# Choosing batch 0's expert from summed state rows, and re-spacing the side work, in a fused attention and switch-routing kernel

## The chip, the cores and the metric

The kernel runs on one NeuronCore of one Trainium2 chip. The metric is the device time of one execution in microseconds (us); the time before is the median of three runs. A profile is one execution recorded by the hardware profiler; its times count from the first instruction of the program.

## The reference

Two blocks follow each other. The first is a two-way cross attention between 512 tokens `x` and 32 states per batch and head (8 batches, 8 heads, 64 channels). Its result, 544 rows of 512 channels per batch, goes into a mixture of 8 experts in which every row uses one expert.

```python
# attention, per batch and head
a  = softmax(x @ state.T / 8);   xread = a  @ state     # 512 rows
a2 = softmax(state @ x.T / 8);   sread = a2 @ x         #  32 rows
rows = concat([xread, sread])                           # (8, 544, 512) -> 4352 rows

# experts
logits = rows @ w_gate                                  # 512 x 8
e      = argmax(logits);  g = softmax(logits)[e]
out    = g * (relu(rows @ w1[e]) @ w2[e])               # w1: 512 x 1024, w2: 1024 x 512
```

Everything is float32.

## The kernel before

With these inputs the 512 token rows of a batch all go to one expert, so the kernel runs a dense two-layer product per batch with one expert's weights. (A branch at the end repairs batches where that does not hold.) The first layer is shortened: a token row is a mixture of 32 states, so the states are multiplied by `w1` first (`G`), and the softmax weights `aT` by `G` (`up`). Then comes `down`, the product with `w2`; from batch 3 on it is done in seven products of half size (`down_by_halves`, products pX, pD, pX, pY, pZ, pW, pD). The 256 state rows go to different experts; they are sorted by expert in groups of 32, and handled at the end in three "rounds" of four groups, with weights of their own (tiles `s`).

Batch 0 has nothing to hide behind, so the order of its first steps matters. `begin()` finds its expert:

```python
load_states(0, sp, act)            # rows 0:32 of st2 by SyncE, rows 32:64 (halves swapped) by ScalarE
load_x(0, sp)
wg = const.tile([128, NDC, E], FP32)
act.dma_start(out=wg[:], in_=moe_w_gate...)      # 512 pieces of 32 bytes
load_states(1, sp, sp)
...
def begin():
    turn_states(0, act.copy)       # VectorE transpose of st2, copy to the other 64 partitions
    states_gates(0)                # pg: gates of each state; ScalarE copies them into gst
    pr = bank("prg")[:, 0:E]
    for g in range(2):             # sum over the states, spread to all partitions
        pe.matmul(pr, lhsT=ones_f[:], rhs=gst[:, 0, g, 0:E], ...)
    xt, sx = new_xt(), new_sx()
    turn_x(0, xt, slice(0, 4))     # VectorE transposes of x, first four heads
    most(0, pr)                    # max, where is it, its number -> eb
    e = expert_of(eb, 0)           # SyncE reads the number into a register
    at_once(w1_parts(0, e, 2))     # 2 x 1 MB
    at_once(w2_parts(0, e))        # 4 x 512 KB
    ...
    turn_x(0, xt, slice(4, 8))
    pc = scores(0, xt)
    ...                            # softmax of the first half on VectorE, ending in aT[0]
    G = states_w1(new_G(), w1s[0], stG[:, 0])    # needs w1
    ...
    up(G, aT[0], hT, one)
```

Each engine runs its instructions in program order. While TensorE works on a batch, the side work (the next batches' attention, then the sorting, then the rounds) is cut into steps by `yield`, and one step is taken at each *slot*. A slot comes after every second piece of `up` (four a batch), twice in each of the four parts of `down` (eight a batch), and after each of the seven products of `down_by_halves`:

```python
def with_weights():
    while True:
        next(work, None)           # one step of the side work
        if lazy:
            lazy.pop(0)()          # one 512 KB part of the weights of the batch after next
        yield

def others():
    ...                            # batches 1 to 7: attention and gates
    yield from sort_states()
    change_pools()
    yield from rounds(0, NRS)

def rounds(r0, r1):                # NDC = 4, NFC = 8, S1B = 4 and S2B = 3 buffers
    ...
    round_experts(r0)
    fetch(2, 0)                    # weights of k = 0
    yield
    yield
    round_in(r0)                   # xg: the sorted rows
    fetch(S1B - 2, S2B)            # k = 1, and three parts of the second layer
    for _ in range(3):
        yield
    for r in range(r0, r1):
        round_x(r)                 # transposes of xg (ptx)
        if r + 1 < r1:
            round_experts(r + 1)
            round_in(r + 1)
        yield
        for k in range(NDC):
            round_up(r, k)         # pgh
            fetch(2, 0)            # two more loads, into the buffers just freed
            yield
            if k < NDC - 1:
                yield
        round_relu(r)
        yield
        round_h(r)                 # transposes (pth)
        yield
        for f in range(0, NFC, 2):
            for i in range(2):
                round_down(r, f + i)   # pgy
                fetch(0, 1)
            yield
            if r + 1 < r1 or f < 4:
                yield
        round_out(r)
```

Of the kernel before, what the change touches and what calls it, by code (L numbers as in the profile page):

```python
# [9 lines left out]
FP32 = mybir.dt.float32  # L10
# [10 lines left out]
def kernel(  # L21
# [32 lines left out]
    pe, dve, act, gp, sp = (InOrder(e) for e in (nc.tensor, nc.vector, nc.scalar, nc.gpsimd, nc.sync))  # L54
# [4 lines left out]
    E = moe_w_gate.shape[1]  # L59
# [7 lines left out]
    NDC = DM // 128  # L67
# [11 lines left out]
    const = ctx.enter_context(tc.tile_pool(name="const", bufs=1))  # L79
# [9 lines left out]
    att = tc.alloc_tile_pool(name="att", bufs=1)  # L89
# [3 lines left out]
    def load_x(b, q):  # L93
        x_nat[b] = att.tile([128, H, NC, D], FP32, tag="x", bufs=2, name="x_nat")
        for h in (slice(0, 4), slice(4, 8)):
            q.dma_start(out=x_nat[b][:, h].rearrange("p h c d -> p h (c d)"),
                        in_=x[b, h].rearrange("h (p c) d -> p h (c d)", c=NC))

    st2 = {}

    def load_states(b, q0, q1):

        rows = state[b].rearrange("h n d -> n h d")
        to = st2[b] = att.tile([64, H, D], FP32, tag="st", bufs=2, name="st2")
        q0.dma_start(out=to[0:32], in_=rows)
        for u in range(2):
            q1.dma_start(out=to[32:64, :, ts(u, 32)], in_=rows[:, :, ts(1 - u, 32)])

    load_states(0, sp, act)
    load_x(0, sp)  # L110
    wg = const.tile([128, NDC, E], FP32)
    act.dma_start(out=wg[:], in_=moe_w_gate.rearrange("(c p) e -> p c e", p=128))
    load_states(1, sp, sp)
    warm = const.tile([128, 1], FP32)
    dve.memset(warm[:], 0.0)
# [13 lines left out]
    dve.tensor_scalar(U128[:], colf[:], iota_p[:, 0:1], None, ALU.is_gt)  # L129
    ones_b = const.tile([128, 128], BF16)  # L130
    gp.memset(ones_b[:], 1.0)
    ones_f = att.tile([128, 128], FP32, name="ones_f")
    gp.memset(ones_f[:], 1.0)
    rev8 = const.tile([128, E], FP32)
    gp.iota(rev8[:], pattern=[[-1, E]], base=E, channel_multiplier=0,
# [50 lines left out]
    gst = att.tile([128, B, 2, 32], FP32, name="gst")  # L186
# [10 lines left out]
    def bank(name):  # L197
        return ps_p.tile([128, 512], FP32, tag="p", name=name)
# [3 lines left out]
    def turn_x(b, xt, h):  # L202
        dve.transpose(xt[:, h].rearrange("p h c u t -> p (h c u t)"),
                      x_nat[b][:, h].rearrange("p h c d -> p (h c d)"))

    def turn_states(b, copy):

        stT[b] = att.tile([128, H, 2, NS], FP32, tag="stT", bufs=2, name="stT")
        to = stT[b][:].rearrange("p h u n -> p (h u n)")
        dve.transpose(to[0:64], st2[b][:].rearrange("p h d -> p (h d)"))  # L210
        copy(to[64:128], to[0:64])
        for g in range(2):
            gp.tensor_copy(out=stG[ts(g, 64), b], in_=stT[b][:].rearrange("p (q g) u n -> p g u q n", g=2)[ts(g, 64), g, 0])

    def states_gates(b):

        pg = [bank("pg") for _ in range(2)]
        for q in range(4):
            for g in range(2):
                pe.matmul(pg[g][ts(q, 32), 0:E], lhsT=stT[b][ts(g, 64), 2 * q + g, 0, :],  # L220
                          rhs=wg[ts(g, 64), q, :], start=True, stop=True, skip_group_check=True)
        for g in range(2):
            act.copy(gst[:, b, g, 0:E], pg[g][:, 0:E])
# [51 lines left out]
    def new_xt():  # L275
        return att.tile([128, H, NC, 2, 32], FP32, tag="xt", bufs=2, name="xt")

    def new_sx():
        return att.tile([128, 4, NB, NS], FP32, tag="sx", bufs=2, name="sx")
# [139 lines left out]
    def most(b, pr):  # L419
        m = att.tile([128, 1], FP32, tag="c_m", bufs=2, name="c_m")  # L420
        dve.tensor_reduce(m[:], pr, AX.X, ALU.max)
        cc = att.tile([128, E], FP32, tag="c_cc", bufs=2, name="c_cc")
        dve.scalar_tensor_tensor(cc[:], pr, m[:], io8[:], ALU.is_ge, ALU.mult)
        dve.tensor_reduce(eb[:, b:b + 1], cc[:], AX.X, ALU.max)

    def begin():

        nonlocal G, hT
        turn_states(0, act.copy)
        states_gates(0)  # L430
        pr = bank("prg")[:, 0:E]
        for g in range(2):
            pe.matmul(pr, lhsT=ones_f[:], rhs=gst[:, 0, g, 0:E], start=(g == 0), stop=(g == 1), skip_group_check=True)
        xt, sx = new_xt(), new_sx()
        turn_x(0, xt, slice(0, 4))
        most(0, pr)
        e = expert_of(eb, 0)
        at_once(w1_parts(0, e, 2))
        at_once(w2_parts(0, e))
        for r in range(NR):  # L440
            sp.dma_start(out=ss_dram[ts(r, 128)], in_=blank[:])
        turn_x(0, xt, slice(4, 8))
        pc = scores(0, xt)
        one, two = slice(0, 2), slice(2, 4)
        soft[0] = (sx,)
        turn_scores(pc, sx, 0)
        turn_scores(pc, sx, 1)
        less_max(sx, one, dve)
        exponential(sx, one)
        load_x(1, act)  # L450
        turn_scores(pc, sx, 2)
        turn_scores(pc, sx, 3)
        over_sum(sx, one, dve)
        turn_read(0, one)
        G = states_w1(new_G(), w1s[0], stG[:, 0])
        less_max(sx, two, dve)
        exponential(sx, two)
        nm = write_max(pc)
        over_sum(sx, two, dve)
        turn_read(0, two)  # L460
        hT = new_hT()
        up(G, aT[0], hT, one)
        soft[0] += write_weights(pc, nm)
        xt, sx = new_xt(), new_sx()
        turn_x(1, xt, slice(0, 4))
        turn_x(1, xt, slice(4, 8))
        turn_states(1, act.copy)
        exps, gates = logits_x(0)

        def beside():  # L470
            states_gates(1)
            pc = scores(1, xt)
            for i in range(4):
                turn_scores(pc, sx, i)
            less_max(sx, ALL, dve)
            nm = write_max(pc)
            yield
            exps()
            gates()
            count(0)  # L480
            turn_write(0)
            write_rows(0)
            exponential(sx, ALL)
            soft[1] = (sx,) + write_weights(pc, nm)
            over_sum(sx, ALL, dve)
            turn_read(1)
            yield
        up(G, aT[0], hT, two, beside(), 4)

    def expert_of(table, i, engines=(SP,)):  # L490
        _, (e,) = nc.values_load_multi_w_load_instructions(
            table[0:1, i:i + 1], engines=list(engines), min_val=0, max_val=E - 1,
            skip_runtime_bounds_check_because="the table holds experts' numbers")
        return e
# [3 lines left out]
    def w1_parts(b, e, cols=1):  # L498

        t = w1s[b] = wpool.tile([128, NDC, F], FP32, tag="w1", name="w1t")  # L500
        rows = moe_w1[ds(e, 1)].rearrange("o (c p) f -> p (o c) f", p=128)
        f = F // cols
        return [lambda k=k: sp.dma_start(out=t[:, :, ts(k, f)], in_=rows[:, :, ts(k, f)]) for k in range(cols)] if cols > 1 else \
            [lambda k=k: sp.dma_start(out=t[:, k], in_=rows[:, k]) for k in range(NDC)]
# [6 lines left out]
    def at_once(parts):  # L511
        for p in parts:
            p()
# [333 lines left out]
    def rounds(r0, r1):  # L847
        need1.extend((r, k, half) for r in range(r0, r1) for k in range(NDC) for half in range(2))
        need2.extend((r, f) for r in range(r0, r1) for f in range(NFC))
        round_experts(r0)  # L850
        fetch(2, 0)
        yield
        yield
        round_in(r0)
        fetch(S1B - 2, S2B)
        for _ in range(3):
            yield
        for r in range(r0, r1):
            round_x(r)
# [5 lines that stand above are left out]
                round_up(r, k)  # L865
                fetch(2, 0)
                yield
                if k < NDC - 1:
                    yield
            round_relu(r)  # L870
            yield
            round_h(r)
# [3 lines that stand above are left out]
                    round_down(r, f + i)  # L876
# [5 lines that stand above are left out]
# [21 lines left out]
    turned, lazy = {}, []  # L903
# [46 lines left out]
    def with_weights():  # L950

        while True:
            next(work, None)
            if lazy:
                lazy.pop(0)()
            yield

    slots = with_weights()
# [11 lines left out]
    with tc.If(number(rest_i, B * S + NG) > 0):  # L970
# [3 lines left out]
        with tc.If(number(left_i, B * S) > 0):  # L974
# [18 lines left out]
            with tc.For_i(0, n_pairs, 1):  # L993
# [14 lines left out]
                e = expert_of(px, 0)  # L1008
# [5 lines left out]
                             in_=at_dram[ds(bb, 1)].rearrange("o p s -> p (o s)"))  # L1014
# [59 lines left out]
```

## Time and profile before

| What | Before |
|---|---|
| device time, median of three (lowest to highest) | 475.73 us (475.02 to 476.54) |
| span of the profiled execution | 473.7 us |
| VectorE busy | 178.0 us (38%) |
| ScalarE busy | 122.1 us (26%) |
| GpSimd busy | 87.3 us (18%) |
| HBM read, written | 94.13 MB, 14.95 MB (230 GB/s over the span) |
| weights of the rounds (`s`): transfers, size, time to landing | 192, 256 KB, 5.3 us |
| weights of the batches (`w1t`, `w2t`): time to landing | 6.3 us |

How to read the lines: PE is a matmul on TensorE and PEld its weight load, DVE is VectorE, ACT is ScalarE, POOL is GpSimd, SP is SyncE; a q behind the name is the engine's sequencer, for instance where it issues a transfer. A line of a timeline gives the start and the length in us, engine, source line, operation, tiles (written <- read), shapes, and how many instructions were merged (x16). In brackets stands the idle time of the engine before it and what ended that, as far as it could be inferred. A float32 matmul leaves two records. A line of the windows gives a stretch, its length, busy time of PE, PEld, DVE, ACT and POOL, the share of the full TensorE clock that was granted, the busy share of the DMA engines and GB/s. A line of the waits gives who waited for whom: total us, times, longest.

All instructions stand under one source line (L48), a helper; the tiles tell them apart. Those that matter here: `stT` transposed states, `pg` and `gst` gates of the states, `prg` their sum, `eb` the expert's number, `pG` and `G` states times w1, `ph` the first layer, `ptx`, `pgh`, `pth`, `pgy` the rounds' steps, `yh` results of the batches from 3 on, `xg` the rounds' rows.

### The profile page before, as it was taken

The numbers are of one execution on the slowest core, as the hardware profiler recorded it, in microseconds if no ns is written. First come the engines' busy times: TensorE is split into PE (matmuls) and PEld (weight loads), VectorE is DVE, ScalarE is ACT, GpSimd is POOL, SyncE is SP. The second block draws the span as 40 slices with busy tenths as digits, with TensorE's granted clock in tenths as the row PEclk, the third lists the DMA queues.
The fourth block names the chain that finished last, engine by engine and source line by source line (L and its number), as shares of the span: only waits on it lengthen the run. The fifth ranks groups of instructions, "written<-read, shape, count | busy, mean of one in ns | idle before, by whom it ended". The sixth has DMA issues, their size and how long they took to land. (4 is left out here: it accounts for less than half of the span.)

```text
span 473.7 us, 9475 instructions
## 1 busy us (share of the span) xinstructions
PE 444.4 (94%) x3685; PEld 250.9 (53%) x3685; DVE 178.0 (38%) x442; ACT 122.1 (26%) x267; POOL 87.3 (18%) x75
## 2 busy tenths in 40 slices
PE   2699899999899999998989999999999999999994
PEld 1386544455455544444637446653766366735762
DVE  4657564757366471402132121422132032402151
ACT  1254233434243443132200312012130222024100
POOL 2000130312212230050224002240224004310220
PEclk9999999999999999999989999999999999999998
DMA  4960497384937422299978899689958997720671
GB/s 114 365 212 22 157 299 268 111 263 142 296 116 260 150 82 95 85 300 397 396 226 307 286 378 403 218 253 392 369 187 298 346 404 229 238 79 1 230 260 56
DMA packets 68258, 110.03 MB, mean 232 GB/s; under 512 B 12783, under 2 KB 27119, under 8 KB 68208
## 3 DMA queue, kind: packets, MB, share of 16 engines
q1 hardware_dynamic: 58512, 98.79, 60.5%
q10 hardware_dynamic: 9296, 9.52, 5.9%
q0 software_dynamic: 400, 1.05, 0.6%
q8 instruction: 31, 0.51, 0.4%
q14 instruction: 19, 0.16, 0.1%
HBM read 94.13 MB, written 14.95 MB: 230 GB/s over the span
## 5 line engine op out<-in xcount | busy, mean ns | idle before, releaser
L48 PE MATMUL py<-w2t,hT 128*128 128x512 f32 x192 | 87.6, 601 | 0.9 <-issue 0.8
L48 PE MATMUL ph<-aTl,G 128*128 128x512 f32 x160 | 71.2, 597 | 0.0
L48 ACT ACTIVATE hT<-ph 128x512 f32<-128x512 f32 (+1 forms) x72 | 39.3, 550 | 120.2 <-PE ph L48 120.0
L48 PEld LDWEIGHTS py<-w2t,hT 128*128 128x128 f32 x192 | 34.8, 190 | 39.8 <-issue 39.1
L48 POOL TENSOR_TENSOR Ta<-w2t,Ta 128x1024 f32<-128x1024 f32 x10 | 24.9, 2491 | 160.4 <-PE pD L48 124.5
L48 PEld LDWEIGHTS ph<-aTl,G 128*128 128x128 f32 x160 | 29.7, 190 | 39.4 <-issue 39.1
L48 PE MATMUL ph<-aTe,G 128*128 128x256 f32 (+1 forms) x128 | 44.8, 500 | 0.0
L48 PE MATMUL pX<-w2t,hT 128*128 128x256 f32 x160 | 36.9, 384 | 0.0
L48 PEld LDWEIGHTS pX<-w2t,hT 128*128 128x128 f32 x160 | 29.7, 190 | 9.5 <-issue 5.0
L48 PEld LDWEIGHTS ph<-aTe,G 128*128 128x128 f32 x128 | 23.9, 194 | 16.1 <-issue 13.7
L48 DVE TENSOR_TENSOR Sa<-hT 128x256 f32<-128x256 f32 x20 | 8.2, 424 | 61.8 <-ACT hT L48 50.7
L48 PE MATMUL pgh<-s,sxT 128*32 128x512 f32 x192 | 26.0, 603 | 2.1 <-DMA s<-in_moe_w_dram 2.1
L48 ACT ACTIVATE yh<-pX,gw 128x256 f32<-128x256 f32 x30 | 12.0, 474 | 56.6 <-PE pX L48 56.6
L48 DVE SCALAR_TENSOR_TENSOR yh<-pY,gw,yh 128x256 f32<-128x256 f32 x20 | 8.3, 478 | 47.4 <-PE pY L48 38.0
L48 PE MATMUL pgy<-s,shT 128*32 128x512 f32 x192 | 25.8, 599 | 0.0
L48 PE MATMUL pG<-w1t,stG 64*32 64x512 f32 x256 | 19.4, 655 | 4.1 <-DMA w1t<-in_moe_w_dram 4.1
L48 ACT COPY G<-pG 128x512 f32<-128x512 f32 x32 | 16.9, 593 | 22.3 <-PE pG L48 22.3
L48 ACT ACTIVATE y<-py,gw 128x512 f32<-128x512 f32 x12 | 8.3, 688 | 54.8 <-PE py L48 54.8
L48 DVE STREAM_TRANSPOSE xt<-x_nat 128x1024 f32<-128x1024 f32 x16 | 19.7, 1232 | 2.9 <-DMA x_nat<-in_x_dram 2.9
L48 DVE STREAM_TRANSPOSE sx<-pc 128x256 f32<-128x256 f32 x32 | 11.7, 419 | 24.2 <-PE pc L48 24.2
L48 PE MATMUL pc<-xt,stT 32*32 32x128 f32 x1024 | 17.0, 295 | 3.0 <-issue 1.6
L48 PE MATMUL pZ<-Tb,Sb 128*128 128x256 f32 x80 | 19.1, 392 | 0.0
(148 smaller groups left out, 499.0 us busy)
## 6 DMA issues: line engine op xcount, KB each, us to landing
s<-in_moe_w_dram SPq DMA_DIRECT2D x192, 256.0 KB, 5.3
w2t<-in_moe_w_dram SPq DMA_DIRECT2D x32, 512.0 KB, 6.3
w1t<-in_moe_w_dram SPq DMA_DIRECT2D x28, 512.0 KB, 6.3
x_nat<-in_x_dram SPq DMA_DIRECT2D x14, 512.0 KB, 5.0
out_dram<-yh ACTq DMA_DIRECT2D x20, 256.0 KB, 4.5
out_dram<-y ACTq DMA_DIRECT2D x12, 256.0 KB, 5.3
at_dram<-aTl SPq DMA_DIRECT2D x5, 512.0 KB, 2.9
w1t<-in_moe_w_dram SPq DMA_DIRECT2D x2, 1024.0 KB, 5.2
```

Of the source, the lines that this page charges most:

```text
L48: ins = getattr(self.engine, name)(*args, **kw)
```

## The change

It has three parts.

1. Batch 0's expert is found earlier in the chain. The sum of the gates is the gates of the sum. So the rows of the states, as loaded, are summed by four small products with a column of ones, and the four columns of sums, spread to 128 columns, are multiplied by the gate weights. That gives the same eight sums without the transposed states. The gate weights are loaded first on ScalarE's queue. The transposes and gates of the states, which the attention still needs, come after it.
2. Where more than four parts of the batches' weights are queued, a slot issues two.
3. The rounds start two slots later after their first loads, and the last round gives these two slots back by leaving out two blank ones in its first layer.

```diff
+    wg = const.tile([128, NDC, E], FP32)
+    act.dma_start(out=wg[:], in_=moe_w_gate.rearrange("(c p) e -> p c e", p=128))
     load_states(0, sp, act)
     load_x(0, sp)
-    wg = const.tile([128, NDC, E], FP32)
-    act.dma_start(out=wg[:], in_=moe_w_gate.rearrange("(c p) e -> p c e", p=128))
     load_states(1, sp, sp)
...
-    ones_f = att.tile([128, 128], FP32, name="ones_f")
+    ones_f = att.tile([128, 1], FP32, name="ones_f")
...
     def begin():
+        ps = bank("pss")[:, 0:4]
+        for q in range(4):
+            pe.matmul(ps[:, q:q + 1], lhsT=st2[0][0:32, ts(q, 2), :].rearrange("p h d -> p (h d)"), rhs=ones_f[0:32],
+                      start=True, stop=True, skip_group_check=True)
+        sums = att.tile([128, 4], FP32, name="sums")
+        dve.tensor_copy(out=sums[:], in_=ps)
+        pr = bank("prg")[:, 0:E]
+        for q in range(4):
+            pe.matmul(pr, lhsT=sums[:, q:q + 1].to_broadcast([128, 128]), rhs=wg[:, q, :], start=(q == 0), stop=(q == 3),
+                      skip_group_check=True)
+        most(0, pr)
         turn_states(0, act.copy)
         states_gates(0)
-        pr = bank("prg")[:, 0:E]
-        for g in range(2):
-            pe.matmul(pr, lhsT=ones_f[:], rhs=gst[:, 0, g, 0:E], start=(g == 0), stop=(g == 1), skip_group_check=True)
         xt, sx = new_xt(), new_sx()
         turn_x(0, xt, slice(0, 4))
-        most(0, pr)
         e = expert_of(eb, 0)
...
         round_in(r0)
         fetch(S1B - 2, S2B)
-        for _ in range(3):
+        for _ in range(5):
             yield
...
                 fetch(2, 0)
                 yield
-                if k < NDC - 1:
+                if k < NDC - 1 and (r + 1 < r1 or k < 1):
                     yield
...
             next(work, None)
-            if lazy:
-                lazy.pop(0)()
+            for _ in range(2 if len(lazy) > 4 else 1):
+                if lazy:
+                    lazy.pop(0)()
             yield
```

## The prediction

> **What bounds the kernel now.** I read the page's busy times first: TensorE is busy 444.4 us of 473.7 and nothing else comes near, so only time in which TensorE waits can be won. The chain of waits is no help (two pieces at the very end, on GpSimd). So I went through TensorE in order of time and looked for gaps, and for groups that last longer than the same group elsewhere.
>
> ```profile
> PE 444.4 (94%) x3685; PEld 250.9 (53%) x3685; DVE 178.0 (38%) x442; ACT 122.1 (26%) x267; POOL 87.3 (18%) x75
> ```
>
> First the opening, from the timeline of its first 26 us (start, length, engine, operation, and in brackets the idle time before):
>
> ```profile
> 1.73 0.52 ACTq L48 DMA_DIRECT2D wg<-in_moe_w_gate_dram  x1
> 5.52 0.70 DVE L48 STREAM_TRANSPOSE stT<-st 64x512 f32<-64x512 f32 x1 [1.86 <-DMA st<-in_state_dram]
> 7.49 0.32 PE L48 MATMUL pg<-wg,stT 64*32 64x8 f32 x16 [7.49 <-DVE xt L48]
> 8.20 0.99 PE L48 MATMUL prg<-gst,ones_f 128*128 128x8 f32 x4 [0.39 <-ACT gst L48]
> 9.77 0.16 DVE L48 TENSOR_REDUCE eb<-c_cc 128x1 int32<-128x8 f32 x1
> 10.65 1.00 SPq L48 DMA_DIRECT2D w1t<-in_moe_w_dram  x2
> 15.95 2.08 PE L48 MATMUL pG<-w1t,stG 64*32 64x512 f32 x16 [2.12 <-DMA w1t<-in_moe_w_dram]
> 18.73 0.71 DVE L48 STREAM_TRANSPOSE aTe<-sx 128x512 f32<-128x512 f32 x1
> 19.96 1.96 PE L48 MATMUL pG<-w1t,stG 64*32 64x512 f32 x16 [1.94 <-DMA w1t<-in_moe_w_dram]
> 21.85 4.35 PE L48 MATMUL ph<-aTe,G 128*128 128x256 f32 x16
> ```
>
> The reader sees a chain: states, transpose, gates, sum, expert (eb, ready at 9.93), weights issued at 10.65, and both halves of pG waiting for them. VectorE's softmax ends its first half (aTe) at 19.44, so up() waits for weights, by 2.4 us. The gates do not wait for stT (ScalarE's copy of it ended at 6.88): their start at 7.46 fits the gate weights landing, which were issued last on ScalarE's queue. That they are named as waiting for xt is, I think, a mislabel.
>
> Next the middle, from TensorE's timeline:
>
> ```profile
> 203.41 10.46 PE L48 MATMUL ph<-aTl,G 128*128 128x512 f32 x24
> 216.01 0.63 PE L48 MATMUL ptx<-ident,xg 128*128 128x128 f32 x4 [2.13 <-DMA w1t<-in_moe_w_dram]
> ...
> 240.15 1.91 PE L48 MATMUL pgh<-s,sxT 128*32 128x512 f32 x12
> 242.33 1.05 PE L48 MATMUL pgh<-s,sxT 128*32 128x512 f32 x2 [0.27 <-DMA s<-in_moe_w_dram]
> 245.24 1.92 PE L48 MATMUL pgh<-s,sxT 128*32 128x512 f32 x2 [1.86 <-DMA s<-in_moe_w_dram]
> 247.08 4.38 PE L48 MATMUL pZ<-Tb,Sb 128*128 128x256 f32 x16
> ...
> 277.01 3.57 PE L48 MATMUL pgy<-s,shT 128*32 128x512 f32 x16
> ...
> 350.45 1.15 PE L48 MATMUL pth<-ident,sh 128*128 128x128 f32 x8 [0.73 <-ACT G L48]
> ```
>
> A step of the rounds (pgh or pgy, 16 records) takes 1.85 us elsewhere, from start to next start (228.96 to 230.81). Here 240.15 to 247.08 is 6.93: 5.1 lost, though the gaps add up to 2.1. After it pZ takes 4.22 to the next start against 3.56 in the next batch: 0.7 more. So this one late load costs 5.7 us. The pgy at 277.01 takes 3.50: 1.65 hidden in "busy". Why the load is late stands in SyncE's waits from 196 to 262 us and in the windows:
>
> ```profile
> SPq L48 <- DMA out_dram<-yh: 9.8, 2, 5.4
> 246.00:248.00 2.00, 2.00 (x4) 0.83 (x3) 0.00 (x0) 0.00 (x0) 0.00 (x0) 0.50 0.95 298
> ```
>
> SyncE waited 5.4 us for a store of batch 3's result (yh) before it could issue the seventh of eight parts of that load: transfers share a few semaphores in turn, and a new one waits until the last user of its semaphore has landed. And the granted clock fell to 0.50.
>
> **What the Trainium skill says.** "TensorE: Matmul & The Clock Gate", section "What's actually happening": the clock is halved by default and released after a busy window of about 3.4 us, and taken back after an idle one. The trace agrees with half speed: pG runs at 1.06 us per matmul at 16 us and 0.60 at 234 us, and the window above shows 0.50 after a wait of only 1.9 us, shorter than the page would lead one to think. "DMA: Bandwidth & Descriptors", section "Queues, rings and completion order": each DMA engine takes turns between queue rows, in ring order within a row. So 512 small pieces of gate weights behind two state loads on one queue land last; issued first, they land first. Same page, section "Latency and other measured facts": a register load has a floor of about 600 ns; here the load of eb takes 0.47 us, and eb's end to the first weight issue is 0.72.
>
> **The change part by part.**
>
> *Opening.* The expert no longer goes through transpose, copy, gates and their eviction. New chain: the first state rows are issued at 0.76, as before; I estimate they can be used at 3.4. Then four products of 32 rows by 128 columns with one moving column: 8 records. The old prg pair made 4 records of 128 columns in 0.99 us, 0.25 each on the cold clock, so 8 take 2.0: 5.4. A copy out (0.15, plus a handover of 0.1): 5.65. By then the gate weights are in: they move ahead of two ScalarE issues of 0.43 and 0.49 us and of the bytes in front of them. Four products with the broadcast sums, 8 records, 2.0: 7.65. The three small operations of most() take 0.70 as before: 8.35. Issue 0.72 later: 9.05 instead of 10.65. Gain 1.6.
>
> What it costs: the gates and scores still need the transposes, and most() now stands before them in VectorE's order. turn_states (0.70) starts at 8.35, the two x transposes (1.2 each) end at about 11.4 instead of 11.08. aTe moves from 19.44 to about 19.8, still before pG's new end (21.9 - 1.6 = 20.3). The second half of the softmax is wanted only when up()'s 32 records (7.8 us) are through. So the 1.6 arrive in full.
>
> *Slots.* A slot is one step of the side work between TensorE groups. Batches 0 to 2 have 12 each, 3 to 6 have 11, batch 7 has 7: 87. Counting the yields, round 0 opens (ptx) in slot 35, which is where the trace has it: third of the four slots of up() for batch 3. A round takes 18 slots, and the last round ends in slot 87. After: ptx in 37, and the last round's up part loses two slots (blanks after k=1 and k=2), so its relu and all after it stay where they were. The loads' issue (slot 32) does not move.
>
> - ptx: wanted two groups later (a ph pair 3.6, pX 3.7), 221 in the old clock; xg landed at 216. Gain 2.1.
> - The late load (k=2): wanted in slot 42 instead of 40. From the end of the second pX, which releases the store that SyncE waits for, TensorE now has pG 1.0, pY 3.6, pG 1.0, k=1 1.9, pZ 3.6, pW 3.6 = 14.7 us before it. The store lands 5.3 after pX's end; two to four parts issued at 0.5 each and 5 us to land make some 12.3. So it should fit, 2.4 to spare. Gain 5.7.
> - The pgy pair at 277: its slot moves to where only pX and pD (7.2) stand between it and the pair before. Its part can be refilled about 6.4 after release (as at the end of the kernel, where such a pair shows 1.1 of wait), under load later. I count 1.0 of the 1.65.
> - pth's 0.73 (waits for ScalarE's G copy, as PSUM is shared): round_h leaves that slot, but the third round's ptx comes to batch 6's fourth product, right behind pG, in the same banks. Net 0.
> - With the waits gone, batch 4's pG comes 3.6 us earlier against the loads, at 230.9 of the old clock. Its last w1t part was issued at 224.19, and the landing time there is 8.0 us (median of three): 0.7 lost, say.
>
> *Two parts a slot.* Only over four queued: from slot 9, and once in each of batches 3 to 5 as w2 joins the end of w1. No wait for w1t or w2t stands in the trace after 20 us but ptx's, which I read as xg's. Worth 0 by itself; it moves the semaphore turns.
>
> Sum: 1.6 + 2.1 + 5.7 + 1.0 - 0.7 = 9.7. The tail (last matmul at 467.05 to 473.7) does not change. The old kernel has three late loads in the rounds (5.7, 1.65, 1.1), by the accident of which transfer shares whose semaphore; every turn is reshuffled, so I set 1.5 aside for new ones. 475.7 - 8.2 = 467.5.
>
> **Rivals.** (1) The wait moves: after the reshuffle another load shares a semaphore with a store that ends late. For it: SyncE waits for yh stores 21.7 us in six places, and the last round's k=1, 2, 3 now stand in three slots running, with batch 6's stores among their loads. Against: between k=0 and k=2 TensorE still has 16 us. Cost 2 to 6 us: 470 to 473. (2) The transfers are the bound, and the wait is only deferred: from 204 to 234 us the DMA share is about 1.0 at 370 to 400 GB/s. Then ptx's gain comes back at pG or k=2: 470. Against: the share falls to 0.2 at 238 to 240, so there was room. (3) The opening gains nothing, as 16 small cold records cost what transpose and copy did: most() ends at 9.9, the transposes move back 1.8 us, and the softmax becomes the bound. 469 to 470. (4) The small products are quicker than cold prg (few rows, one column): 2.5 instead of 1.6, capped by aTe: 466.6.
>
> **Range and chances.** Middle 467.5. The opening can be 0 to 2.5, the slots 3 to 9. Range 463.8 to 472. Two per cent is 9.5 us (466.2), which needs nearly the whole sum without a new wait: faster 0.40, same 0.58, slower 0.02.
>
> **What would show it.** Right: eb's last operation at about 8.2 and w1t's issue at 9; ptx without a gap; the third pgh of round 0 at 1.85 us and no clock of 0.50 after the opening; a gap of 0.7 before the third round's ptx. Wrong: up() starting on aTe instead of pG; a pgh or pgy of over 3 us at another place, with SyncE waiting for yh; pG in batch 3's slots waiting for w1t by over 1 us.

## The result, and the profile after

| | Before | After |
|---|---|---|
| device time, median of six (lowest to highest) | 474.77 us (472.6 to 476.54) | 468.25 us (467.61 to 470.19) |
| span of the profiled execution | 473.7 us | 468.4 us |

The ratio is 0.9868 with a 95% interval of 0.9836 to 0.9899: 6.3 us faster (4.8 to 7.8). The prediction was 8.2. The two profiles differ by 5.3 us, and the lines below say where. The page's busy times of the changed kernel first; TensorE's busy time has not fallen, so the gain is all waits.

```profile
PE 444.9 (95%) x3697; PEld 254.1 (54%) x3697; DVE 178.0 (38%) x443; ACT 121.9 (26%) x267; POOL 87.3 (19%) x75
```

The opening, from the timeline of the changed kernel's first 31 us:

```profile
0.75 0.45 ACTq L48 DMA_DIRECT2D wg<-in_moe_w_gate_dram  x1
2.96 1.83 PE L48 MATMUL pss<-ones_f,st 32*128 32x1 f32 x8 [2.96 <-DMA st<-in_state_dram]
5.05 1.87 PE L48 MATMUL prg<-wg,sums 128*128 128x8 f32 x8 [0.26 <-DVE sums L48]
7.51 0.16 DVE L48 TENSOR_REDUCE eb<-c_cc 128x1 int32<-128x8 f32 x1
7.62 0.70 DVE L48 STREAM_TRANSPOSE stT<-st 64x512 f32<-64x512 f32 x1
8.40 1.00 SPq L48 DMA_DIRECT2D w1t<-in_moe_w_dram  x2
17.77 1.96 PE L48 MATMUL pG<-w1t,stG 64*32 64x512 f32 x16 [2.14 <-ACT G L48]
18.23 0.71 DVE L48 STREAM_TRANSPOSE aTe<-sx 128x512 f32<-128x512 f32 x1
19.66 8.85 PE L48 MATMUL ph<-aTe,G 128*128 128x256 f32 x32
```

The expert is known 2.3 us earlier and the weights go out 2.25 us earlier (8.40 against 10.65). up() starts 2.2 us earlier, but its 32 records now run to 28.44, where they ran to 29.59: only 1.15 us are left. The granted clock is released at 23.1 us in both profiles, so the earlier start was spent on the half clock.

The middle, from TensorE's timeline of the changed kernel:

```profile
224.66 0.60 PE L48 MATMUL ptx<-ident,xg 128*128 128x128 f32 x4
...
239.84 1.92 PE L48 MATMUL pgh<-s,sxT 128*32 128x512 f32 x16
241.70 3.72 PE L48 MATMUL pZ<-Tb,Sb 128*128 128x256 f32 x16
...
279.93 2.60 PE L48 MATMUL pgy<-s,shT 128*32 128x512 f32 x16
...
394.71 0.66 PE L48 MATMUL ptx<-ident,xg 128*128 128x128 f32 x4 [0.73 <-ACT G L48]
```

No gap before ptx, no late load at what is now k=1 (k=2 at 248.80 takes 1.86 as well), 2.53 to the next start instead of 3.50 for the pgy pair, and the 0.73 moved to the third round's ptx. From the first ph of batch 3 to the last pD the old kernel needs 259.9 us (203.41 to 463.33), the new one 250.5 (207.48 to 457.96): 9.4 less.

That leaves a loss. At the first ph of batch 3 (203.41 before, 207.48 after) the new kernel is 4.07 us *behind*, after being 1.15 ahead at 28. Of these 5.2 us, 0.7 are lost at batch 1's pG and 4.5 in batch 4's attention (the products pc). From the same timeline:

```profile
120.18 1.85 PE L48 MATMUL pc<-xt,stT 32*32 32x128 f32 x123
125.64 0.64 PE L48 MATMUL pc<-xt,stT 32*32 32x128 f32 x5 [3.60 <-issue]
126.21 5.02 PE L48 MATMUL py<-w2t,hT 128*128 128x512 f32 x8
```

and the same place before the change:

```profile
120.61 1.90 PE L48 MATMUL pc<-xt,stT 32*32 32x128 f32 x128
122.44 3.27 PE L48 MATMUL py<-w2t,hT 128*128 128x512 f32 x7
126.47 0.70 PE L48 MATMUL py<-w2t,hT 128*128 128x512 f32 x1 [0.76 <-issue]
```

TensorE stands for 3.6 us for "issue": nothing that the profile shows held it. After that the clock is at half speed (the window of the changed kernel from 126 us), and eight py records take 5.0 us instead of 3.6:

```profile
126.00:128.00 2.00, 2.00 (x7) 0.84 (x3) 1.64 (x5) 0.00 (x0) 0.00 (x0) 0.50 0.07 22
```

From pc's start to the next pG this stretch takes 10.98 us against 6.49: 4.5 lost. It is in no step of the prediction, and one of its signs of being right, no clock of 0.50 after the opening, did not come.

**A theory for the gap.** It moved by a fixed number of instructions: from 7 py records behind pc to 5 pc records before its end. That is 12 matmuls and 12 weight loads, just what the opening adds (x3685 became x3697). Both kernels have one more such gap, 1.6 us in batch 2's pc. Between the two gaps each has 887 matmuls and 887 weight loads. These are the windows between the gaps, of the changed kernel and of the one before:

```profile
58.20:125.50 67.30, 62.67 (x887) 32.53 (x887) 37.53 (x84) 23.51 (x57) 15.02 (x15) 1.00 0.73 238
```

```profile
59.40:126.40 67.00, 65.75 (x887) 33.57 (x887) 40.19 (x89) 23.64 (x57) 16.03 (x16) 1.00 0.69 224
```

With the 18 semaphore instructions that the trace records on TensorE there, that is 1,792 = 7 x 256. The transfers on the instruction queue are 31 of 16,384 bytes each (the page's queue line, and the transfers themselves in the trace):

```profile
q8 instruction: 31, 0.51, 0.4%
```

The Trainium skill, "Runtime: NRT & Kernel Launch", section "Instruction fetch mechanics", says that an engine's instructions are refilled in blocks of 16 KiB, which are 256 instructions, and calls the cost of crossing a block limit mostly hidden. The count agrees; the hiding does not hold here. A pc of 128 records and 128 weight loads is just such a block and runs in 1.85 us. Counted from the gaps, the block before the long gap is entered at 120.04. There is no instruction transfer from 120 to 123.1, and then one in the stretch from 123.1 to 123.4:

```profile
q8 instruction: 1, 0.02, 21.2%
```

TensorE goes on at 125.64. So, by this theory, a block that is used up in less than some 4.3 to 5.6 us (what such blocks last in the two gaps) leaves TensorE waiting for the next. Before the change that block held seven slow py pairs besides pc; now it holds nothing but small products.

### The profile page after: what moved, and what is told of

Its sections match the earlier page's. It is cut to its first block, busy times and chain, and to the rows that moved or that the text cites. A ratio compares the mean times of both kernels' runs of the same rounds, so it can differ in the third digit from the quotient of the medians.

```text
span 468.4 us, 9501 instructions
## 1 busy us (share of the span) xinstructions
PE 444.9 (95%) x3697; PEld 254.1 (54%) x3697; DVE 178.0 (38%) x443; ACT 121.9 (26%) x267; POOL 87.3 (19%) x75
## 5 line engine op out<-in xcount | busy, mean ns | idle before, releaser
L48 PE MATMUL py<-w2t,hT 128*128 128x512 f32 x192 | 88.6, 607 | 0.5 <-ACT hT L48 0.4
L48 PE MATMUL ph<-aTe,G 128*128 128x256 f32 (+1 forms) x128 | 45.9, 510 | 0.0
L48 PE MATMUL pgy<-s,shT 128*32 128x512 f32 x192 | 24.5, 599 | 0.0
L48 PE MATMUL pgh<-s,sxT 128*32 128x512 f32 x192 | 23.1, 598 | 0.0
L48 PE MATMUL pY<-Ta,Sa 128*128 128x256 f32 x80 | 18.6, 386 | 0.0
```

The source lines that it names most:

```text
L48: ins = getattr(self.engine, name)(*args, **kw)
```

## The experiments

Ratios are to the kernel before, run beside each. The theory is the one of instruction pages (blocks); a rival stands in nearly every expectation.

**The opening alone.** The diff of the first part of the change, nothing else.

> Only the first part of the change (expert from summed rows, gate weights first). Theory (instruction pages): TensorE's instructions come in pages of 256; the opening adds 24 of them, so the page limit that lay 7 pairs into batch 4's py moves back into the fast pc products, where the next page cannot come in time. Expected: a TensorE gap of about 3.6 us marked issue inside a pc of 128 at about 122 us, a slow clock after it, and the kernel 2 to 4 us slower than before although up() ends 1.1 us earlier. Rival (the long gap of the profile was chance, or came from the shifted rounds or the doubled slots): no gap over 1 us there, and 1 to 2 us faster than before.

Measured: 474.23 against 472.84 us, ratio 1.0026 (1.0003 to 1.0049): 1.2 us slower. The gap is at the same record. From TensorE's timeline of this kernel:

```profile
120.10 1.86 PE L48 MATMUL pc<-xt,stT 32*32 32x128 f32 x123
124.25 0.41 PE L48 MATMUL pc<-xt,stT 32*32 32x128 f32 x5 [2.29 <-issue]
124.59 5.40 PE L48 MATMUL py<-w2t,hT 128*128 128x512 f32 x8
```

So neither the doubled slots nor the rounds make it. The loss is a little smaller than expected, as is the gap. One thing the theory did not foresee: the other gap, in batch 2's pc, does not come here. The changed kernel had, from its TensorE timeline,

```profile
58.22 0.48 PE L48 MATMUL pc<-xt,stT 32*32 32x128 f32 x23 [1.64 <-issue]
```

and the opening alone has

```profile
56.56 2.28 PE L48 MATMUL pc<-xt,stT 32*32 32x128 f32 x128
58.77 3.70 PE L48 MATMUL py<-w2t,hT 128*128 128x512 f32 x8
```

So the place of a gap is fixed by the count, but whether it comes is not. Counted as above, the block of this pc is entered at 55.44 in the opening alone and its instruction transfer starts 0.7 us later; in the changed kernel it starts 1.85 us after the entry.

**The rounds alone.**

```diff
-        for _ in range(3):
+        for _ in range(5):
...
-                if k < NDC - 1:
+                if k < NDC - 1 and (r + 1 < r1 or k < 1):
```

> Only the third part (rounds two slots later, last round closer). Theory: no instruction is added, so no new gap at 122 us, and the whole gain of the middle shows: 9.2 us (ptx 2.1, the late load of k=2 5.7, pgy 1.0, last pgy 0.4), ratio 0.980 to 0.982. Rival (the middle gains less, and the two other parts bring the rest): 5 us or less, ratio 0.99.

Measured: 466.21 against 472.84 us, ratio 0.9862 (0.9815 to 0.9909): 6.5 us faster, between the two. Its profile shows the whole 9.3 us between the first ph of batch 3 and the last pD (204.70 to 455.34), and no gap at 122 us. So the middle gains what it shows; the likely reason for the 6.5 is that the kernel before costs less on average than in my one profile. The third pgh of round 0 lost 5.1 us there. It loses 2.6 in the opening alone, 2.9 in the padded opening below and 1.8 in the doubled slots alone, all with the old rounds. This is the step in the opening alone (242.81 to 247.29, where 1.85 would do):

```profile
242.81 2.94 PE L48 MATMUL pgh<-s,sxT 128*32 128x512 f32 x14
246.31 1.05 PE L48 MATMUL pgh<-s,sxT 128*32 128x512 f32 x2 [0.56 <-DMA s<-in_moe_w_dram]
247.29 3.72 PE L48 MATMUL pZ<-Tb,Sb 128*128 128x256 f32 x16
```

**Twelve idle pairs in the kernel before.** Tiny products on a constant, ahead of TensorE's first real one, read by nobody; no other part of the change.

```diff
+        pad_b = bank("pad")
+        for i in range(12):
+            pe.matmul(pad_b[ts(i % 4, 32), 0:1], lhsT=pad_t[ts(i % 4, 32), 0:32],
+                      rhs=pad_t[ts(i % 4, 32), 0:1], start=True, stop=True, ...)
         turn_states(0, act.copy)
```

> The kernel before with 12 tiny matmuls (24 TensorE instructions) in TensorE's idle time ahead of its first real one; nothing reads them. Theory (instruction pages): the same gap of about 3.6 us at about 123 us and 4 to 5 us slower than before, ratio 1.008 to 1.010. Rival (the gap has to do with the transfers or with the opening's time): same as before, ratio 0.999 to 1.001.

Measured: ratio 1.0086 (1.0053 to 1.0120): 4.1 us slower for 24 instructions that take 0.25 us of idle time. From its TensorE timeline (one of its longer executions, so only the place of the gap is read from it):

```profile
0.97 0.25 PE L48 MATMUL pad<-pad_t 32*32 32x1 bf16 x12 [0.97 <-DVE warm L48]
122.62 1.85 PE L48 MATMUL pc<-xt,stT 32*32 32x128 f32 x123
127.07 0.41 PE L48 MATMUL pc<-xt,stT 32*32 32x128 f32 x5 [2.60 <-issue]
```

The gap falls on the very record of the changed kernel, though nothing of the opening has changed. So the rival is out as the reason for the gap and its place; its length is another matter: it is 3.60 and 3.43 us in the two profiles of the changed kernel and 2.29 in the opening alone.

**116 idle pairs in the changed kernel.** 58 before the sums, 58 before most(); 232 + 24 = 256, so the block limits return to where they were.

> The changed kernel with 116 tiny matmuls (232 instructions) in TensorE's idle time of the opening, half before the sums, half after the gates' sum, so that with the change's own 24 the pages end where they ended before the change. Theory: the gap at 122 us shrinks from 3.6 to about 0.8 and the clock stays full; 3 to 4.5 us faster than the changed kernel, about 464. Rival: the gap stays, and the kernel is 0 to 1 us slower for the extra instructions.

Measured: 465.40 against 472.84 us, ratio 0.9847 (0.9797 to 0.9898). The changed kernel did not run beside it; through the kernel before, this is about 1 us better than the change, and the intervals overlap, so the gain of 3 to 4.5 us is not shown. The place is shown. Its TensorE timeline:

```profile
118.75 1.90 PE L48 MATMUL pc<-xt,stT 32*32 32x128 f32 x128
120.58 2.84 PE L48 MATMUL py<-w2t,hT 128*128 128x512 f32 x6
124.93 1.12 PE L48 MATMUL py<-w2t,hT 128*128 128x512 f32 x2 [1.51 <-issue]
```

The gap is back in py and less than half as long, and the clock stays full.

**The changed kernel again, and with 99 pairs.** 99 was chosen from the trace as near the best place of the limits.

> The changed kernel once more, as it is, so that the padded ones have it on the same chip. Every theory: ratio 0.985 to 0.989 to the kernel before; a TensorE gap marked issue of 2 to 4 us in batch 4's pc.

> The changed kernel with 99 idle tiny matmuls (198 instructions) in the opening. From the trace of the changed kernel, with a page lasting at least 4.3 to 5.6 us before the next can begin, this is near the best place of the page limits: the two gaps (1.7 and 3.6 us) come down to 1.4 to 3.8 us together. Theory (pages): 3 to 4 us faster than the changed kernel run beside it, and 0 to 1 us faster than with 116 pairs. Rival (any shift does the same, or the pads help by warming the clock): not better than with 116 pairs, or the gaps stay as they are.

Measured side by side: the changed kernel 469.34 us, ratio 0.9887 (0.9841 to 0.9932), with its gap of 3.43 us; with 99 pairs 466.95 us, ratio 0.9845 (0.9798 to 0.9891). 2.4 us between the medians, less than expected, and the intervals overlap, so that the gain itself is not clear of noise. The gaps in batches 2 and 4 are gone, and a new one is in batch 0's pc. From the timeline of the kernel with 99 pairs:

```profile
11.20 1.99 PE L48 MATMUL pc<-xt,stT 32*32 32x128 f32 x74 [0.44 <-DVE xt L48]
15.44 1.30 PE L48 MATMUL pc<-xt,stT 32*32 32x128 f32 x38 [2.25 <-issue]
...
122.53 1.90 PE L48 MATMUL pc<-xt,stT 32*32 32x128 f32 x128
124.37 3.70 PE L48 MATMUL py<-w2t,hT 128*128 128x512 f32 x8
```

With the pads, a block of the opening consists of small, fast instructions alone: the last pads, the gates and most of this pc. TensorE also waits there for aTe, and up()'s 32 records end at 32.60 instead of 28.40: what the pads save in batches 2 and 4 they partly cost here.

**The opening with the limits put back.** The first part of the change with 116 pairs.

> The opening alone (first part of the change) with 116 idle tiny matmuls, so that pages end as before the change. Theory: the opening alone was 1.2 us slower only by the page limit, which cost 4.1 us in the kernel before with 12 pairs; so this one is 1.1 to 2.9 us faster than before, ratio 0.994 to 0.998. Rival (the opening itself gains nothing, or loses): ratio 1.000 to 1.003.

Measured: 471.14 against 474.10 us, ratio 0.9929 (0.9907 to 0.9951): 3.4 us faster, a little more than expected. The same opening without pads was 1.2 us slower: about 4.6 us between the two, for 232 instructions that do nothing. Not all of the 3.4 need be the opening: the late load is cheaper in its profile (2.9 instead of 5.7).

**Stores on GpSimd's queue.** Is the late load late because of the shared semaphore (the counter by which an engine learns that a transfer has landed)?

```diff
         def store(y, i, k):
-            no_dep(act.dma_start(out=rows[:, ts(i, 2), ts(k, 256)], in_=y[:]))
+            no_dep(gp.dma_start(out=rows[:, ts(i, 2), ts(k, 256)], in_=y[:]))
```

> The kernel before, only the yh stores (batches 3 to 7) are issued on GpSimd's queue, whose transfers have semaphores of their own. Theory (the late load of k=2 waits because it shares a semaphore with a yh store): SyncE no longer waits for yh, the third pgh of round 0 takes 1.85 us, 4 to 6 us faster than before (ratio 0.987 to 0.992). Rival (the transfers' rate is the bound, the semaphore only the last in line): the third pgh stays over 4 us, ratio 0.997 to 1.003.

Measured: ratio 0.9925 (0.9889 to 0.9961): 3.5 us faster, with the rounds' slots as they were. Its TensorE timeline at the late load:

```profile
240.59 1.92 PE L48 MATMUL pgh<-s,sxT 128*32 128x512 f32 x16
242.45 3.72 PE L48 MATMUL pZ<-Tb,Sb 128*128 128x256 f32 x16
```

The load comes in time though it is wanted as early as before, and SyncE's waits from 196 to 262 us no longer name yh. So the rate of the transfers was not the bound; the turn of the semaphore was. The experiment changes queue and semaphore at once, but the trace of before has the semaphores: the transfers of SyncE and ScalarE share eight, and the yh store issued at 235.44 has the same one as the load issued at 239.74, when SyncE's wait ended. GpSimd's transfers have others. The 3.5 us are under the expected 4 to 6, and not the late load's alone: the pgy pair that took 3.50 takes 1.85 here as well (280.68 to 282.53).

**Two parts a slot alone.**

```diff
-            if lazy:
-                lazy.pop(0)()
+            for _ in range(2 if len(lazy) > 4 else 1):
+                if lazy:
+                    lazy.pop(0)()
```

> Only the second part (two weight parts a slot over four queued). Theory: no TensorE wait stood on these loads after the opening, no instruction is added on TensorE, so no difference: ratio 0.998 to 1.002, the late loads in the rounds perhaps at other places. Rival (it makes part of the middle's gain): 1 to 3 us faster.

Measured: ratio 1.0040 (1.0023 to 1.0058): 1.9 us slower, which neither expected. In the profile the wait before ptx is longer, and this time it pulls the clock down (0.54 from 217 to 219 us):

```profile
217.72 1.09 PE L48 MATMUL ptx<-ident,xg 128*128 128x128 f32 x4 [2.81 <-DMA s<-in_moe_w_dram]
218.60 4.59 PE L48 MATMUL ph<-aTl,G 128*128 128x512 f32 x8
```

Here ptx and the eight ph last 1.4 us longer than in the profile of before. But the rounds as a whole take no longer in it than there, so whether this is the 1.9 us stays open. In the changed kernel the wait is gone with the later slot.

**Three attempts at a better kernel.** First the 99 pairs between the two halves of batch 0's pG; then also the stores on GpSimd; then also ten products of 128 by 512 on a constant in TensorE's idle times of the opening (89 pairs remain).

> The changed kernel with the 99 tiny pairs between the two halves of batch 0's pG, where TensorE waits for weights. In the opening of the kernel with 99 pairs further ahead a page limit fell into batch 0's pc and cost 2.7 us. Theory (pages): here neither the opening nor batches 2 and 4 have a gap marked issue of over 1 us; 4 to 6 us faster than the changed kernel, ratio to before 0.975 to 0.980. Rival (the pads cost what they save): 0.984 to 0.987 as with the pads ahead.

> The same, and the yh stores on GpSimd's queue. Theory: in the changed kernel the late load of k=2 is gone anyway, so the stores' own semaphores can only take the short pgy waits left (0.7 at 280 us, 0.8 to 1.7 at 455 us): 0 to 1.5 us faster than without. Rival (semaphore sharing still costs elsewhere): 3 us or more.

> The same, and TensorE's idle time of the opening filled with ten products of 128 by 512 that nothing reads, so that the clock is released before up() begins instead of 3.4 us after. Theory (up() starts on the half clock): up()'s first 32 records take 7.2 us instead of 8.8, another 1.5 to 2.5 us faster. Rival (the clock's window falls by chance, or the fill delays the real products): no difference, or slower.

| Kernel | Median | Ratio (95%) |
|---|---|---|
| before, beside them | 473.37 us | |
| 99 pairs between pG | 466.15 us | 0.9856 (0.9808 to 0.9903) |
| and stores on GpSimd | 464.65 us | 0.9821 (0.9788 to 0.9855) |
| and the fill | 466.90 us | 0.9883 (0.9831 to 0.9935) |

The first comes out at its rival's ratio, not at the 0.975 to 0.980 of the theory. It keeps batches 2 and 4 free of gaps, but again a limit finds a run of fast instructions, now among the pads (its TensorE timeline):

```profile
14.99 0.51 PE L48 MATMUL pad<-pad_t 32*32 32x1 bf16 x46
18.24 0.55 PE L48 MATMUL pad<-pad_t 32*32 32x1 bf16 x53 [2.74 <-issue]
18.73 2.14 PE L48 MATMUL pG<-w1t,stG 64*32 64x512 f32 x16
```

The second has the lowest ratio of all, 8.5 us (6.9 to 10.0) under the kernel before and, through it, some 2 us under the change; it did not run beside the change, and their intervals overlap. The third does what it was made for and gains nothing that can be measured. In its TensorE timeline up() runs at full clock, and later waits appear:

```profile
19.47 7.14 PE L48 MATMUL ph<-aTe,G 128*128 128x256 f32 x32
26.55 0.65 PE L48 MATMUL pl<-aTe,gst 128*32 128x128 f32 x16
27.12 2.86 PE L48 MATMUL ph<-aTe,G 128*128 128x256 f32 x12
31.16 1.13 PE L48 MATMUL ph<-aTe,G 128*128 128x256 f32 x4 [1.18 <-DVE lg L48]
```

The 32 records take 7.1 us instead of 8.8. Then TensorE waits 1.2 us, and batch 1's pG loses 2.9 us on w1t instead of the second kernel's 1.9: both profiles stand at 68.6 when it begins.

## Why the prediction came out as it did

- *Opening, 1.6.* Right on average, and by luck in part. The chain was shorter than worked out: sums at 2.96, not 3.4, products 1.85 each, not 2.0, so 2.25 us at the weights' issue. Against that I left out that up() would start on the half clock. In the profiles without a page gap in the opening, up()'s 32 records end at 28.44, 28.40, 30.13, 28.42 and 28.07 with the new opening, at 29.59, 31.31, 31.00 and 30.30 with the old: 1.9 us between the means. That they "arrive in full" holds only for these means, not in each execution. In three of the five TensorE waits for aTe by 0.4 to 2.8 us (2.75 in the opening alone, where the state rows that ScalarE's queue loads came 1 us later); so up() starting on aTe, one of the prediction's signs of being wrong, came there, and rival 3's softmax bound is near. That the gates waited for the gate weights, as guessed, and not for xt is borne out: the rounds alone, with the old opening, name wg at that wait. And batch 1's pG, behind w1t, took 0.7 us back in the changed profile.
- *ptx, 2.1.* Right: 2.13 before, no gap after.
- *The late load, 5.7.* The mechanism (a shared semaphore with a yh store) is shown by the stores' own experiment. The term is mis-sized: I read it off one profile. In three others with the old rounds the same step lost 1.8 to 2.9; the mean of the four is 3.3. With 2.1, 3.3 and 1.0 the middle comes to 6.4, and the rounds alone brought 6.5.
- *pgy pair, 1.0; pth and ptx, 0.* Right: of 1.65 there is 0.68 left, and 0.73 moved as said.
- *Batch 4's pG, -0.7.* It did not come in this profile; 0.4 in the rounds alone.
- *Two parts a slot, 0.* Not confirmed: slower by 1.9 alone.
- *Put aside for new waits, 1.5.* This is the step that failed. I looked for new waits among loads and semaphores ("every turn is reshuffled"). The new wait came from the number of instructions: 24 more of them alone cost 4.1 us, shown with 12 idle pairs, and the gap moved back when 232 more put the limits back.

The number came out near, but the two large errors do not cancel: both made the forecast too good. The late load was counted about 2.5 us too dear, and the block limit, 4.1, was not counted at all. Taking both from the sum of 9.7 leaves 3.1, while 6.3 (4.8 to 7.8) and, in the second comparison, 5.4 (3.2 to 7.5) were measured. The 1.5 put aside made up for a part, for a reason that it was not meant for. The averages of the parts do no better: opening 1.9, rounds 6.5, block limits -4.1 give 4.3 us, or 2.4 if the 1.9 that the doubled slots lose alone is taken off too. The intervals are wide (the rounds' 4.3 to 8.7, the limits' 2.5 to 5.7), so the difference may be noise, or the parts may not add up; that stays open. That the result lies within the range is in part luck.

## What to carry to other kernels

Where a stretch runs hundreds of tiny matmuls at some 7 ns an instruction, count instructions, not only time: here TensorE got them in blocks of 256, and adding or removing a few anywhere earlier can move a block limit into that stretch and cost microseconds, which the timeline shows only as "issue". When a load is late although the transfer engines have room, look at which transfer used its semaphore last; a queue with semaphores of its own was worth 3.5 us here, without any change of order. And size a wait from several executions: the same late load cost between 1.8 and 5.7 us here.

## What the runs showed of the hardware

- Every gap of TensorE over 0.7 us that is marked "issue" comes, to within one, after the same count of its recorded instructions, 193 and a multiple of 256: after the 1,473rd and the 3,265th in the kernel before, in the one with 12 pairs, and in both profiles of the changed one. The count fixes the place, not whether a gap comes: the opening alone has none at the 1,473rd, the rounds alone none at the 3,265th.
- Blocks of 256 that last 5.9 to 6.1 us by their own work show no gap in any profile. Blocks with a gap were stretched to 3.3 to 6.6 us, and one of 2.5 us passed without. The long gap follows how late the instruction transfer starts after the block is entered: 3.2 us in both profiles of the changed kernel (gaps of 3.60 and 3.43), 1.8 in the opening alone (2.29). What delays the transfer is not shown.
- Waits of 1.9 us (before), 2.3 (opening alone), 2.8 (doubled slots) and 3.6 (changed) were each followed by the half clock, while a wait of 2.13 us before ptx was not. "TensorE: Matmul & The Clock Gate", section "What's actually happening" of the Trainium skill has the idle window at about 3.4 us and free-running. In the trace of before, the half clock lasts 3.41 us, from 245.04 on, and about 1.9 of the 3.41 us ahead of that were idle: here a window idle for a little over half was enough. Counting back from 245.04 in steps of 3.41, an estimate, such a window ends within the wait before ptx, and the next one holds 1.7 us of it, which is half of the window.
